# Mamba-2 scan and PReLU block: last six pairs of chunks cut into chunks of 64 tokens, with a pair's outputs, the next pair's gram and its state products in one visit of TensorE

## The chip, the cores and the metric

The kernel runs on one core of one Trainium2 chip. The metric is the device time of one execution in microseconds (us), the median of the runs shown. Before the change three runs took 355.93, 356.24 and 357.10 us, so the median is 356.24 us.

TensorE is the matmul engine (PE in the profile, its weight loads PEld), VectorE is DVE, ScalarE is ACT, GpSimd is POOL, and SyncE (SP) issues most of the DMAs. PSUM is the memory that matmuls write. [...]

## The reference

There are 4 batches, 8 heads, 768 tokens, a head dimension D of 32 and a state dimension N of 16. For each head a decayed linear attention is computed, then all tokens go through a two-layer block with a PReLU:

```python
for c in range(nc):                      # chunks of 32 tokens
    cum = cumsum(log(clip(a)))           # in the chunk
    L = exp(cum_i - cum_j) * (i >= j)
    y_intra = ((C @ B.T) * L) @ x        # the gram C B^T, decayed
    y_inter = (C @ state) * exp(cum)
    state = exp(sum(la)) * state + sum_j(exp(cum_last - cum_j) * B_j x_j)
x = y.transpose(0, 2, 1, 3).reshape(3072, 256)
h = x @ w_in                             # 256 -> 2048
out = (max(h, 0) + alpha * min(h, 0)) @ w_out    # 2048 -> 256
```

The result does not depend on the length of a chunk. A kernel may take 128 or 64 tokens: the work inside a chunk (gram, decay, product with x) grows with its length, and each chunk needs one state at its beginning.

## The kernel before

**Tiling.** The 3072 tokens are 24 chunks of 128 (`Q`), or 12 pairs of chunks (`gp` is 0 to 11, `NP = 12`, three pairs to a batch). Two pairs make a group of 512 tokens (`g` is 0 to 5), the unit of the two-layer block. The scan of a pair has to leave its result, the tile `xT` of its group, before the block begins with that group. The kernel therefore works on group g of the block while it scans the pairs of group g+1 (`nxt = 2g + 2`).

**The block.** From group 1 on, the block uses seven products in place of eight (a Strassen-like scheme with sums of weights and of tokens). `quad(g, z, after, third)` does a quarter of the hidden units, z = 0 to 3. It writes two PSUM tiles, A and Y, from the pool `ps_h`, which has two buffers. A "third" quad also has a tile Z in the pool `ps_s`. The order on each engine is the order of the Python code, since the schedule is manual. A quad runs: A; Y; A again after ScalarE copied A away to `u2` (L1265); VectorE adds `u2` to Y (L1267); A again and Y again; PReLUs on ScalarE (L1224) and VectorE (L1226); four differences on GpSimd (L1288, L1298). Between these stand fifteen places `after(0)` to `after(14)`. There the products of the previous quad with `w_out` (`product`, L1216) and the steps of the scan are put. The tables `with_gram` and `without` (L1502 to 1504) give the places of the products, and `steps` (L1487) those of the scan. At z = 0 from g = 2 on, `combine` joins the products of the group before. Its last two VectorE steps (L1322, L1323) and the two GpSimd steps behind them (L1325, L1326) stand at `after(14)`.

**The scan of a pair.** `pair(gp)` is a generator whose steps are called by `ssm`. In order:

- `added` or `added_halves` multiplies the state input (`bn`, B times its decays, made on GpSimd at L533) with x.
- `states` (L642) carries the state over. GpSimd spreads it over the heads (L645).
- `scan_half` (L561, L567) makes the decays L, by a scan on VectorE of the decay rows that a DMA spread over the partitions (`load_spread`, tile `abc`), with an identity matrix as the other operand. That identity lies in half of a PSUM bank whose other half holds product 5 of the block.
- `spread_c` and `c_decayed` (L679, L682) prepare C. For the later pairs `moved` (L690, L692) also brings C and state to the other 64 partitions.
- `products_bc` (L722) makes the gram on TensorE, into two tiles of `ps_s` and two of `ps_h`. VectorE multiplies it with the decays (L753).
- The outputs are matmuls of C with the state (L779) and of x with the decayed gram (L787), and ScalarE copies them to `xT` (L815).

The last six pairs (`gp >= HALF`, which is 6) already work with the array cut into tiles of 64 rows: tokens 0 to 63 and 64 to 127 of a chunk are two "halves" j. The upper half of the gram has 128 columns, the lower half only 64, so a head takes `SQ` = 192 columns.

**Two visits.** TensorE turns to each of these pairs twice. The gram stands at `after(13)` of an even quad (z = 0 or 2). The outputs stand at `after(5)` of the odd quad that follows, between the products of `u2`'s A and the next use of A, and the state products of the next pair come right behind them.

**Buffers.** `ps_s` and `ps_h` have two banks each, `ps_q` four. `lda` (the tiles `abc`) and `ldx` (x, B, C) have three buffers, `work` two, `czp` one.

Of the kernel before, what the change touches and what calls it, by code (L numbers as in the profile page):

```python
# [22 lines left out]
def kernel(  # L23
# [55 lines left out]
    SQ = Q + HQ  # L79
# [69 lines left out]
    def load_spread(gp, b, c):  # L149

        for w, t in enumerate(loads["p", gp][1] if gp >= HALF else ()):
            rows = scratch["z", b // 2].rearrange("(b h c) t -> b c h t", b=2, h=H)
            for k in range(2):
                nc.sync.dma_start(
                    out=t[HQ * k : HQ * (k + 1), : 4 * SQ].rearrange("p (h t) -> p h t", h=4),
                    in_=rows[b % 2, c + k, 4 * w : 4 * w + 4].unsqueeze(0)
                    .to_broadcast([HQ, 4, SQ]))
# [12 lines left out]
    def load_pair(gp, decays=True, parted=False):  # L170
# [47 lines left out]
        for k in range(2 if gp >= NB else 0):  # L218
            abc.append(lda.tile([P, H * Q], F32, name="abc"))
# [201 lines left out]
    def halve_identity():  # L421

        for s in range(2):
            nc.scalar.copy(
                out=ident_p[0][HQ:].rearrange("p (a s t) -> p s a t", a=2, s=2)[:, s],
                in_=ident[HQ:, HQ * (1 - s) : HQ * (2 - s)].unsqueeze(1).to_broadcast([HQ, 2, HQ]))
# [22 lines left out]
    def rows_clamp(i):  # L449
        rows = loads.pop(("r", i))  # L450
        d0 = prep.tile([RW, SQ], F32, name="r0")
# [5 lines left out]
        if i:  # L457
            nc.vector.tensor_scalar(out=d0[:, Q + 1 :], in0=rows[:, HQ + 1 :], scalar1=1e-6,
                                    scalar2=1.0, op0=ALU.max, op1=ALU.min)
        held[i] = d0  # L460

    def rows_scan(i):

        d0 = held[i]
        nc.vector.memset(d0[:, Q : Q + 1], 0.0)
        pr = prep.tile([RW, Q], F32, name="pr")
        nc.vector.tensor_tensor_scan(out=pr[:, ::-1], data0=d0[:, 1 : Q + 1][:, ::-1],
                                     data1=ends[:RW, ::-1], initial=0.0,
                                     op0=ALU.mult, op1=ALU.add)
        return pr  # L470

    def rows_out(i):


        if i == 0:
# [3 lines left out]
        d0 = held.pop(i)[:, :SQ]  # L479
        rpf = prep.tile([RW, Q], F32, name="rpf")  # L480
        nc.vector.tensor_tensor_scan(out=rpf, data0=d0[:, :Q], data1=zeros[:RW], initial=1.0,
                                     op0=ALU.mult, op1=ALU.add)
        nc.vector.memset(d0[:, :1], 0.0)
# [68 lines left out]
    halved = []  # L552

    def scan_half(dec, abc, k, w):
        dv = dec.rearrange("p k h t -> p k (h t)")
        if ident_p and halved:
            dv = dec.rearrange("p k h t -> p (k h t)")
            for i in range(2):
                s = (2 * w + i) * SQ
                o = (4 * k + 2 * w + i) * SQ  # L560
                nc.vector.tensor_tensor_scan(out=dv[:, o : o + SQ], data0=abc[k][:, s : s + SQ],  # L561
                                             data1=ident_p[0][:, :SQ], initial=0.0,
                                             op0=ALU.mult, op1=ALU.add)
            return
# [6 lines left out]
    def turn_bc(gp):  # L571
# [7 lines left out]
        scan_half(decs[gp], loads["p", gp][1], 0, 0)  # L579

    def pair(gp):
# [5 lines left out]
        half = gp >= HALF  # L587
        dec = decs.pop(gp) if gp in decs else work.tile([P, 2, H, Q], F32, name="dec")
        by_head = dec.rearrange("p k h t -> p (k h t)")[:, : H * SQ].rearrange(
            "p (h t) -> p h t", h=H)  # L590
# [15 lines left out]

        shifted = one.tile([P, 2, P], F32, name="shifted") if half else None

        def added_halves(banks):


            dps = [t[:, : 4 * D].rearrange("p (k m) -> p k m", k=2) for t in banks]
            for j in range(2):
                for r in range(4):
                    rs, hs = slice(32 * r, 32 * r + 32), slice(2 * r * D, 2 * (r + 1) * D)
                    for k in range(nk):
                        ks = slice(HQ * k, HQ * (k + 1))
                        nc.tensor.matmul(dps[k][rs, k], bn[ks, j, rs], xt[ks, j, hs],
                                         start=False, stop=j == 1,
                                         tile_position=(HQ * k, 32 * r),  # L620
                                         skip_group_check=True)
            return dps
# [30 lines left out]
        if fine:  # L653
            bn = bns.pop(gp) if gp in bns else pair_loads(gp)
            if half:
                dps = added_halves(beside.pop(gp))
            else:
                dps = added(beside.pop(gp) if gp in beside else ss_tile()[:, : 2 * Q])
# [26 lines left out]
        def moved():  # L685


            for k in range(2):
                to, frm = (slice(HQ * v, HQ * (v + 1)) for v in (k, 1 - k))
                nc.scalar.copy(out=shifted[to, 0], in_=cd[frm, k])  # L690
                if st[k] is not None:
                    nc.gpsimd.tensor_copy(out=shifted[to, 1], in_=st[k][frm])  # L692

# [4 lines left out]
        if fine:  # L698
            for k in range(2):
                for w in range(2):  # L700
# [5 lines left out]
                    if k == 1 and w == 1:  # L706
                        spread_c()
                        c_decayed()
                        if half:
                            moved()  # L710
# [11 lines left out]
        def products_bc():  # L722
            small = 2 if fine else 3
            gram = {r: ss_tile() if r < small else spare() for r in range(4)}
            for j in range(2 if half else 0):
                for r in range(4):
                    rs = slice(32 * r, 32 * r + 32)
                    for k in range(2):
                        o = gram[r][HQ * k : HQ * (k + 1), : 2 * SQ].rearrange(
                            "p (h t) -> p h t", h=2)  # L730
# [849 lines left out]
```

## Time and profile before

| | |
|---|---|
| median of the three runs | 356.24 us |
| the profiled execution | 357.65 us |
| its span, first to last instruction | 355.9 us |
| TensorE matmuls busy | 349.3 us (98%) |
| VectorE busy | 235.8 us (66%) |
| GpSimd busy | 204.4 us (57%) |
| ScalarE busy | 171.8 us (48%) |
| TensorE's share of the chain that ended last | 89% |
| granted TensorE clock | 1.00 |

The profile comes from one execution. A float32 matmul of the program shows as two records, each with its own weight load. A group line reads "line, engine, operation, output<-inputs, shape, xcount | busy us, mean ns". The chain of waits is followed back from the last instruction. In order of time it shows, for each stretch, which instruction was the one that everything later hung on. A busy TensorE is not necessarily an efficient one, so the timeline of the single records is read as well.

### The profile page before, as it was taken

What the parts mean: (1) busy time and instruction counts of PE and PEld (TensorE: products, weight loads), DVE (VectorE), ACT (ScalarE), POOL (GpSimd) and SP (SyncE); (2) the same over time, 40 slices, a digit from 0 to 9 for tenths busy, and PEclk for the clock granted to TensorE, in tenths of its full rate; (3) what the DMA queues carried; (4) which work ended last, traced back from release to release, by engine and by line L of the source; (5) the groups of instructions that cost most, each with busy time, mean ns of one, the idle gap of its engine ahead of it and who ended that gap; (6) DMA issues with size and microseconds to landing.
All of it is one profiled execution on the core that took longest, in us unless ns stands there. A gap on an engine that the chain in (4) does not pass through costs nothing.

```text
span 355.9 us, 7778 instructions
## 1 busy us (share of the span) xinstructions
PE 349.3 (98%) x2985; PEld 284.4 (80%) x2985; DVE 235.8 (66%) x482; ACT 171.8 (48%) x391; POOL 204.4 (57%) x228
## 2 busy tenths in 40 slices
PE   8899999999999999999999999999999999999996
PEld 4576665578788888888888888888888888888885
DVE  6876986998748756847747856757856633643363
ACT  3477576535355346345345445345445344443431
POOL 6776568589939855725646626637526535434520
PEclk9999999999999999999999999999999999999999
DMA  7899989607345403503423423422001001001102
GB/s 138 182 202 270 329 174 279 148 17 159 106 83 128 102 3 75 104 2 77 78 57 74 86 51 71 85 55 65 11 2 31 0 2 29 2 1 31 31 0 59
DMA packets 105581, 30.24 MB, mean 85 GB/s; under 512 B 79896, under 2 KB 101448, under 8 KB 105544
## 3 DMA queue, kind: packets, MB, share of 16 engines
q1 hardware_dynamic: 103048, 29.43, 36.3%
q10 hardware_dynamic: 2496, 0.32, 0.6%
q8 instruction: 23, 0.38, 0.5%
q14 instruction: 14, 0.11, 0.1%
HBM read 26.32 MB, written 3.42 MB: 84 GB/s over the span
## 4 chain that ended last, share of the span: by engine, by line
PE 89%; SPq 4%; DMA 3%; DVE 2%; ACT 1%; POOL 1%; issue 0%; DVEq 0%; ACTq 0%
PE bank L1216 33%; PE hp L1241 29%; PE bank L1142 6%; PE ss L1241 6%; PE hp L1095 3%; DMA raw<-in_moe_w_in_dram 2%; SPq L192 2%; PE ss L787 1%; PE ss L731 1%; PE hp L1110 1%; PE bank L1209 1%; PE ss L805 1%; PE ss L779 1%; DMA xt<-in_x_dram 1%; SPq L197 1%; PE ss L742 1%
## 5 line engine op out<-in xcount | busy, mean ns | idle before, releaser
L1298 POOL TENSOR_TENSOR gt<-gt 128x512 f32<-128x512 f32 x58 | 74.2, 1279 | 21.1 <-DVE gt L1226 16.3
L1216 PE MATMUL bank<-gt,w_out 128*128 128x256 f32 x320 | 83.5, 381 | 0.0
L1216 PEld LDWEIGHTS bank<-gt,w_out 128*128 128x128 f32 x320 | 60.1, 190 | 9.2 <-issue 1.0
L1288 POOL TENSOR_TENSOR gt<-gt 128x512 f32<-128x512 f32 x20 | 25.4, 1269 | 62.5 <-DVE gt L1226 49.7
L1226 DVE SCALAR_TENSOR_TENSOR gt<-hp,s_mul,gt 128x256 f32<-128x256 f32 x96 | 42.0, 479 | 29.1 <-ACT gt L1224 26.8
L1224 ACT ACTIVATE gt<-hp,s_alpha 128x256 f32<-128x256 f32 x96 | 40.3, 471 | 34.5 <-PE hp L1241 31.4
L1216 PE MATMUL bank<-gt,ws 128*128 128x256 f32 x224 | 55.9, 379 | 0.0
L1216 PEld LDWEIGHTS bank<-gt,ws 128*128 128x128 f32 x224 | 42.3, 190 | 5.6
L1241 PE MATMUL hp<-xs,w_in 128*128 128x256 f32 x160 | 41.9, 384 | 0.0
L1241 PE MATMUL hp<-xs,ws 128*128 128x256 f32 x160 | 41.1, 380 | 0.0
L1267 DVE TENSOR_TENSOR hp<-hp,u 128x512 f32<-128x512 f32 x20 | 14.0, 700 | 35.2 <-ACT u L1265 35.2
L1241 PEld LDWEIGHTS hp<-xs,ws 128*128 128x128 f32 x160 | 30.3, 190 | 4.3 <-POOL xs L1183 0.2
L1241 PEld LDWEIGHTS hp<-xs,w_in 128*128 128x128 f32 x160 | 29.7, 190 | 4.5
L1142 PE MATMUL bank<-w_out,gt 128*128 128x256 f32 x128 | 31.1, 385 | 0.4 <-POOL w_out L330 0.4
L1142 PEld LDWEIGHTS bank<-w_out,gt 128*128 128x128 f32 x128 | 23.6, 190 | 7.2 <-issue 2.9
L1241 PE MATMUL ss<-xT,w_in 128*128 128x256 f32 x96 | 24.6, 379 | 0.0
L645 POOL TENSOR_TENSOR sm<-state,bmask 128x256 f32<-128x256 f32 (+1 forms) x10 | 6.2, 620 | 29.0 <-DVE state L642 29.0
L1095 PE MATMUL hp<-xT,w_in 128*128 128x512 f32 x48 | 22.8, 596 | 0.0
L561 DVE TENSOR_TENSOR_SCAN dec<-abc,bank 128x192 f32<-128x192 f32 x48 | 22.7, 522 | 0.0
L1256 ACT COPY m<-hp 128x512 f32<-128x512 f32 x8 | 4.7, 586 | 35.7 <-PE hp L1241 35.7
L1265 ACT COPY u<-hp 128x512 f32<-128x512 f32 x20 | 11.7, 585 | 19.4 <-PE hp L1241 19.4
L1226 DVE SCALAR_TENSOR_TENSOR gt<-c,s_mul,gt 128x256 f32<-128x256 f32 x40 | 20.6, 555 | 0.0
(232 smaller groups left out, 608.2 us busy)
## 6 DMA issues: line engine op xcount, KB each, us to landing
abc<-z SPq DMA_DIRECT2D x24, 192.0 KB
raw<-in_moe_w_in_dram SPq DMA_DIRECT2D x8, 512.0 KB
raw<-in_moe_w_out_dram SPq DMA_DIRECT2D x8, 512.0 KB
abc<-z SPq DMA_DIRECT2D x8, 512.0 KB
out_dram<-o_sb SPq DMA_DIRECT2D x32, 64.0 KB
nat<-in_B_dram SPq DMA_DIRECT2D x26, 64.0 KB
xt<-in_x_dram SPq DMA_DIRECT2D x12, 128.0 KB
xt<-in_x_dram SPq DMA_DIRECT2D x24, 64.0 KB
```

The source lines that it names most:

```text
L192: eng.dma_start(out=nat[:, i, k].rearrange("p (h n) -> p h n", h=H), in_=src[b, :, ts, :].rearrange("h p n -> p h n"))
L561: nc.vector.tensor_tensor_scan(out=dv[:, o : o + SQ], data0=abc[k][:, s : s + SQ], data1=ident_p[0][:, :SQ], initial=0.0, op0=ALU.mult, op ...
L1095: nc.tensor.matmul(hp, w_in[:, k, f * P : (f + 1) * P], xts[g][:, k], start=(k == 0), stop=(k == KC - 1))
L1142: nc.tensor.matmul(pos[0][t // 2][:, t % 2], gt[:, t * Q : (t + 1) * Q], w_out[:, f], start=(f == 0 and t % 2 == 0), stop=(f == NF - 1), s ...
L1216: nc.tensor.matmul(ms[g][i][:, h], w, blocks[g, z][n][:, p], start=(q == 0 and h == 0), stop=(q == NQ - 1), skip_group_check=True)
L1224: nc.scalar.mul(o[:, p], h[:, p], s_alpha[:, fs[p]])
L1226: nc.vector.scalar_tensor_tensor(out=o[:, p], in0=h[:, p], scalar=s_mul[:, fs[p]], in1=o[:, p], op0=ALU.mult, op1=ALU.max)
L1241: nc.tensor.matmul(to[:, p], w(2 * z + p), b, start=start and p == 0, stop=True, skip_group_check=True)
L1265: nc.scalar.copy(out=u2, in_=A)
L1267: nc.vector.tensor_tensor(out=Y, in0=Y, in1=u2, op=ALU.add)
L1288: nc.gpsimd.tensor_tensor(out=tc_, in0=g22, in1=g12, op=ALU.subtract)
L1298: eng.tensor_tensor(out=o, in0=x0, in1=x1, op=ALU.subtract)
```

## The change

Pairs 6 to 11 go from halves of a 128-token chunk to true chunks of 64 tokens.

1. **Shape.** The decay rows restart every 64 tokens (`rows_scan`, `rows_out`). A head has 128 columns per pair instead of 192 per chunk half. A pair needs one tile `abc` and four scans of 128x256 on VectorE instead of two tiles and eight scans of 128x192. The gram of each half has 128 columns, and the four multiplications are 128x256 instead of 128x384.
2. **States.** There are four states per pair. `state_products` has the same sixteen matmuls, with the sums of the two halves no longer added up. `states_four` has up to four VectorE steps. `carried_four` has eight GpSimd operations on 64 partitions each and two ScalarE copies.
3. **One visit.** `visit(gp)` at `after(13)` of an even quad issues the gram of pair gp+1, two of its four multiplications on VectorE, the outputs of pair gp, the copies to `xT`, and the state products of pair gp+1. The outputs are written to the second half of the two `ps_h` banks whose first half holds gram, the state products to the second half of the two `ps_s` banks. `behind(gp)` at `after(1)` of the odd quad issues the other two multiplications and the states; `carried_four` follows at `after(2)`.
4. **Way in.** Quad (1, 3) becomes a third quad. Pair 5 puts its outputs at `after(6)` there, and its `xT` copies come before the state products of pair 6. `carried_four(6)` follows at `after(11)`, and at `after(13)` a visit with the gram of pair 6 alone and two extra matmuls of ones.
5. **Loads.** From pair 7 on, a pair is loaded one pair earlier than before.

The core of the diff, with the parts of the old path that go left out:

```diff
@@ rows_scan / rows_out
+        n = HQ if i else Q
+        for o in range(0, Q, n):
+            nc.vector.tensor_tensor_scan(out=pr[:, o : o + n][:, ::-1],
+                                         data0=d0[:, o + 1 : o + n + 1][:, ::-1],
...
@@ new functions
+    def scan_four(gp, n):
+        cs = slice(2 * Q * n, 2 * Q * (n + 1))
+        nc.vector.tensor_tensor_scan(out=decays_of(gp)[:, cs], data0=loads["p", gp][1][0][:, cs],
+                                     data1=ident_p[0], initial=0.0, op0=ALU.mult, op1=ALU.add)
+    def c_by_head(gp):
+        czs[gp] = czp.tile([P, 2, 2, Q], F32, name="cz")
+        for i in range(2):
+            nc.scalar.mul(czs[gp][:, i].rearrange("p k t -> p (k t)"),
+                          bcs[gp][:, 2:].rearrange("p k t -> p (k t)"), par[:, i : i + 1])
+    def gram_four(gp, banks, begun=()):
+        cz = czs.pop(gp)
+        for j in range(2):
+            js = slice(HQ * j, HQ * (j + 1))
+            for r in range(4):
...
+                for k in range(2):
+                    o = banks[r][HQ * k : HQ * (k + 1), : 2 * Q].rearrange("p (h t) -> p h t", h=2)
+                    nc.tensor.matmul(o[:, :, js], bcs[gp][rs, k, js], cz[rs, :, k, js],
...
+    def decayed(gp, banks, r):
+        o = decays_of(gp)[:, 2 * Q * r : 2 * Q * (r + 1)]
+        nc.vector.tensor_tensor(out=o, in0=banks[r][:, : 2 * Q], in1=o, op=ALU.mult)
+    def states_four(gp, dps):
...
+            nc.vector.scalar_tensor_tensor(out=to, in0=entering[gp][:, s], scalar=ap[:, e : e + 1],
+                                           in1=new, op0=ALU.mult, op1=ALU.add)
+    def carried_four(gp):
...
+        for k in range(2):
+            to, frm = (slice(HQ * v, HQ * (v + 1)) for v in (k, 1 - k))
+            nc.gpsimd.tensor_tensor(out=cs[to, 0], in0=ct[to, k], in1=ap[to, k], op=ALU.mult)
+            nc.gpsimd.tensor_tensor(out=cd[frm], in0=ct[frm, k], in1=ap[frm, k], op=ALU.mult)
+            nc.scalar.copy(out=cs[to, 1], in_=cd[frm])
...
+            for i, rows in enumerate((to, frm)):
+                nc.gpsimd.tensor_tensor(
+                    out=ss[to, i, js].rearrange("p j (g m) -> p j g m", g=2),
+                    in0=ent[rows, 2 * k + js.start : 2 * k + 2].unsqueeze(2)
...
+    def outputs_four(gp, y, fresh):
+        for i in range(2):
+            for j in range(2):
...
+                            nc.tensor.matmul(y[k][qs, k ^ i, js], ss[ks, i, j, qs], cs[ks, i, js],
...
+        for w in range(2):
+            for j in range(2):
...
+                        nc.tensor.matmul(y[k][qs, w, HQ * j : HQ * (j + 1)],
+                                         xt[ks, j, h * D : (h + 1) * D],
+                                         decays_of(gp)[ks, o : o + HQ], start=False, stop=True,
...
+    def visit(gp):
+        nxt = gp + 1
+        banks = {0: ss_tile(), 1: spare(), 2: ss_tile(), 3: spare()}
+        if nxt < NP:
+            begun = (1, 3) if gp < HALF else ()
+            for r in begun:
...
+            gram_four(nxt, banks, begun)
+            for r in (1, 3):
+                decayed(nxt, banks, r)
+        if gp >= HALF:
+            y = [banks[r][:, 2 * Q :].rearrange("p (k t) -> p k t", k=2) for r in (1, 3)]
+            outputs_four(gp, y, nxt >= NP)
...
+            for k in range(2):
+                nc.scalar.copy(out=xts[g][:, :, (q + k) * Q : (q + k + 1) * Q], in_=y[k])
+            if nxt < NP:
+                beside[nxt] = [banks[r][:, 2 * Q :] for r in (0, 2)]
+                state_products(nxt, beside[nxt])
+        visits[gp] = banks
+    def behind(gp):
+        nxt, banks = gp + 1, visits.pop(gp)
+        if nxt < NP:
+            for r in (0, 2):
+                decayed(nxt, banks, r)
+            if gp >= HALF:
+                states_four(nxt, beside.pop(nxt))
@@ order of the steps
+    def thirds(g, z):
+        return 2 * g + 2 >= NP or z % 2 == 0 or (g, z) == (1, 3)
+    def sixth(z, j):
...
+        if (z, j) == (3, 6):
+            state_products(n, beside[n])
+            states_four(n, beside.pop(n))
+        if (z, j) == (3, 11):
+            carried_four(n)
+        if (z, j) == (3, 13):
+            visit(n - 1)
+        if (z, j) == (3, 14):
+            behind(n - 1)
+            turn_bc(n + 1)
+    def fours(gp, odd, j):
...
+        if not odd and j == 13:
+            visit(gp)
+        if odd and j == 1:
+            behind(gp)
+        if odd and j == 2 and gp + 1 < NP:
+            carried_four(gp + 1)
+        if odd and gp + 2 < NP:
+            if j == 5:
+                turn_bc(gp + 2)
+                scan_four(gp + 2, 0)
+            if j in (12, 14):
+                scan_four(gp + 2, 1 if j == 12 else 2)
...
+            late = 6 if (g, z) == (1, 3) else 5
...
+            if z % 2 and j == late and gp < HALF:
+                for p in (0, 1, 0, 1):
+                    ssm(gp + p)
+            if gp == HALF - 1:
+                sixth(z, j)
+            if HALF <= gp < NP:
+                fours(gp, z % 2, j)
+            if z % 2 and j == 9 and gp + (2 if gp < HALF - 1 else 3) < NP:
+                load_pair(gp + (2 if gp < HALF - 1 else 3))
...
-        quad(g, z, after, nxt >= NP or z % 2 == 0)
+        quad(g, z, after, thirds(g, z))
```

## The prediction

> **What bounds the kernel now.** The page comes first: TensorE is busy for 98% of the span, and the chain of waits gives it 89%. The second answer read is the list of TensorE's waits. It names six, 3.1 us together, and all six belong to lines of the start, before group 1. So from group 1 on, where the change lies, TensorE never idles. What is added to its queue, or keeps it waiting, lengthens the kernel; what other engines gain does not count.
>
> ```profile
> PE 349.3 (98%) x2985; PEld 284.4 (80%) x2985; DVE 235.8 (66%) x482; ACT 171.8 (48%) x391; POOL 204.4 (57%) x228
> PE 89%; SPq 4%; DMA 3%; DVE 2%; ACT 1%; POOL 1%; issue 0%; DVEq 0%; ACTq 0%
> ```
>
> Third, the chain in order of time around pair 6 (start, length, what). Four records of a full stream last 0.86 us, 0.216 each.
>
> ```profile
> 144.89 1.29 PE bank L1216 x6
> 146.18 0.38 PE ss L731 x4
> ...
> 147.02 1.06 PE bank L1216 x4
> ...
> 151.53 0.86 PE bank L1216 x4
> 152.40 0.24 PE ss L779 x4
> ...
> 154.13 1.92 PE hp L1241 x8
> ```
>
> The gram takes 146.18 to 147.02, and the first four full records after it 1.06 in place of 0.86: 1.04 us. The outputs with the state products take 152.40 to 154.13, plus 1.92 less 1.73: 1.92 us. Read alike, all six grams cost 1.03 and the outputs of pairs 6 to 11 cost 1.93, 1.86, 1.95, 1.93, 1.86, 1.61 (the last has no state products). Together 6.2 + 11.1 = 17.3 us.
>
> Fourth, the timeline around the gram of pair 7, and around the u copy of the quad behind pair 6's gram.
>
> ```profile
> 173.25 0.45 PE L731 MATMUL ss<-cz,bc 32*64 32x256 f32 x4
> 173.73 0.29 PE L731 MATMUL ss<-cz,bc 32*64 32x128 f32 x4
> 173.84 0.29 PE L731 MATMUL ss<-cz,bc 32*64 32x128 f32 x4
> 173.87 0.29 PE L731 MATMUL hp<-cz,bc 32*64 32x128 f32 x4
> 174.23 1.02 DVE L753 TENSOR_TENSOR dec<-hp,dec 128x384 f32<-128x384 f32 x2 [2.15 <-PE hp L731]
> ```
>
> ```profile
> 148.12 0.42 DVE L1322 TENSOR_TENSOR c<-u,bank 128x256 f32<-128x256 f32 x1
> 148.46 0.42 DVE L1323 TENSOR_TENSOR c<-bank,u 128x256 f32<-128x256 f32 x1
> 151.57 0.58 ACT L1265 COPY u<-hp 128x512 f32<-128x512 f32 x1 [1.14 <-PE hp L1241]
> ```
>
> To be seen: eight array tiles work at once, and a round of 128 columns takes 0.11 us (173.73 to 173.84). VectorE starts 0.07 us after the gram's modelled end. A 128x256 operation on PSUM takes 0.42, the next starts 0.34 after it. The u copy waits for TensorE alone.
>
> [...] weight loads stop for 0.33 us before each visit, of which I count 0.31 as lost. [...] of the last outputs' 1.61 us, 0.31 is the drain and 0.43 the four 128-column rounds of L779; 0.87 is left for the eight rounds of L787, half with 128 columns and half with 64, which is 0.109 each. [...]
>
> **The change part by part.**
>
> *The visit's wait.* The outputs go to the second half of the two banks whose first half holds gram, so as built their first matmul waits for both `decayed(1)` and `decayed(3)`. Queued behind it: the whole of TensorE. From the visit's start: 0.31 drain; the gram's four rounds start at 0, 0.16, 0.27 and 0.38 (the first pair spaced 0.05 wider than its columns, as in L731), plus 0.05 within a round and 0.27 to the end, near 0.69 (bank 1's part 0.66); VectorE starts at 0.74; two multiplications, 0.34 + 0.42, end at 1.49; TensorE follows 0.05 later (VectorE's L887 to TensorE's L929 took that). Resumption at 0.31 + 1.49 + 0.05 = 1.85 us, where the gram's columns alone would end at 0.31 + 0.43. After `combine` (pairs 6, 8, 10) VectorE is at L1319 and L1320 until 147.10, 1.29 after the visit's start, so both multiplications are 0.24 later: 2.09.
>
> *The visit's columns.* State: 32 matmuls of 64 columns (before, 16 of 128); x: 32 of 64 (before, 16 of 128 and 16 of 64); each is 8 rounds counting both passes. At 0.109 a round that is 0.87 + 0.87. State products and way out as before: 1.95 - 1.61 = 0.34. A merged visit costs 1.85 + 2.08 = 3.93, after `combine` 4.17. The bound from below is 0.054 a round, the columns alone, as if rounds were proportional: 0.87 less. I take 0.109, because L787 measures it.
>
> *Sum of visits.* 3 x 4.17 + 2 x 3.93 = 20.4. The last visit has no gram: 0.31 + 0.87 + 0.87 = 2.05. The visit with pair 6's gram alone: 0.31 + 0.43 + 0.43 for the matmuls of ones + 0.13 = 1.30. Together 23.7 against 17.3: **+6.4** (bound below +1.2).
>
> *Pair 5.* Its state products for pair 6 now stand behind the two `xT` copies, in the same bank. Matmul end and handover about 0.3, two copies 0.27 + 0.38, less the drain that is there anyway: **+0.9** (0.5 to 1.1).
>
> *The copies of `carried_four` on ScalarE.* They stand ahead of the u copy (L1265's work), and the next use of A on TensorE waits for that. They wait for GpSimd. Quads behind visits 6, 8 and 10: `combine`'s L1322 needs product 4, which now comes after the whole visit. From the visit's end: product 4 done 1.24; L1322, L1323 end 2.04; GpSimd's L1325, L1326 (0.73 each) end 3.54; then two products 64x128, two 64x256, two 64x128 before the second copy can start. The trace shows no GpSimd product on 64 partitions. I take the time of 128 partitions with the same row length (L645: 0.45 and 0.73), with starts 0.41 and 0.70 apart: 6.58. Copies end 6.95, u copy 7.50. TensorE, through five pieces of 0.86 and product 2, wants A at 5.18: **2.4 us** of idling, 1.8 for pair 9, whose first two spreads are 64x128. Before, this quad had the outputs (1.9 us) in this place. Sum **+6.6**. The bound below is half the GpSimd times: 2.4. Quads behind visits 7, 9, 11 have no `combine`: second copy by 3.95, u copy wanted at 4.73, so no hold; but the u copy ends at 5.32 against 5.18: +0.1 each, **+0.3** (0 to 0.6).
>
> *`carried_four(6)`.* Its copies stand ahead of the next quad's copy from Z to A. GpSimd's last difference (L1298) ends 4.2 after a gram visit's start (150.03 against 145.81), 3.65 without the `bn` step there; six products (four of 64x128) bring the second copy to 6.5, the copy to A to 7.1. TensorE wants A at 1.30 + 3.5 pieces = 4.3: **+2.8** (bound below 1.6).
>
> *At nothing.* Four scans in place of eight, 128x256 in place of 128x384, and fewer DMA bytes all lie on engines and queues with idle time; if that cover went they would be gains of VectorE, not of TensorE. SyncE's loads move a pair earlier, and the buffers they need are freed by the visit before. The third quad (1, 3) has the same matmuls. C's spread on ScalarE delays an even quad's u copy to 4.32, wanted by 4.75.
>
> **Sum:** 6.4 + 0.9 + 6.6 + 0.3 + 2.8 = +17.0 us. The profiled execution took 357.65 (span 355.9), so 374.7 (span 372.9); that execution is 1.4 above the median of 356.24, which gives **373.2 us**.
>
> **Rivals.**
>
> *Short matmuls are cheap.* Rounds of 64 columns at 0.054: 5.2 us less, 368.0. For it: some state products (L618) are that close. Against it: L787. If GpSimd's narrow operations are half as well: 1.2 + 0.5 + 2.4 + 1.6 = +5.7, 362.
>
> *ScalarE's copies hold nothing.* If the GpSimd work before the second copy is short enough, only the visits remain: 373.2 - 6.6 - 2.8 = 363.8. Against it: that would take the six products from 3.0 to some 0.6 us.
>
> *Not slower: TensorE's own work decides.* If VectorE's multiplications were in time, a visit would save one drain, a way out and columns: at 0.054 a round 0.31 + 0.43 + 0.86 + 0.34 = 1.95 against 2.96, so about 5 us in five visits, 351. It decides where the wait inside the visit is shorter than the 1.0 us saved and nothing holds ScalarE. The two multiplications with their handovers alone are 1.1.
>
> **Chances.** The likeliest case 0.60; between it and 364 (one of the first two rivals, or half of each) 0.28; both, 360 to 364, 0.06; the last rival 0.04; no change 0.02. A measurement of this kernel tells about 0.3% from no change (1.1 us): slower 0.94, same 0.02, faster 0.04. The range reaches from 361.5, where all lower bounds meet, to 376.5, with rounds of 64 columns 0.03 dearer than 0.109.
>
> **What would show it.** Right: TensorE waits for VectorE's multiplications in five visits, some 1.1 us each; 16 rounds near 0.11 between resumption and state products; TensorE waits for ScalarE's u copy in three quads, near 2.4 us, and once for the copy to A; ScalarE's copies behind GpSimd. Wrong: no such wait in the list, or the outputs of a visit under 1.5 us. It would fail most if narrow GpSimd products were quick.

## The result, and the profile after

The changed kernel takes **389.76 us** (median of 4 runs, 388.39 to 390.28); the kernel before took 356.31 us beside it. The ratio is **1.093**, 95% interval 1.0896 to 1.0963. The direction was forecast, the size was not: 373.2 us, at most 376.5. The profiled execution took 389.65 us with a span of 387.9, so 32.0 us of span have to be found.

The page of the changed kernel: engines, TensorE's granted clock in 40 slices, instruction queue 8, taken for TensorE's (25 packets for its 3197 records and 3197 weight loads), and the chain.

```profile
PE 357.9 (92%) x3197; PEld 288.6 (74%) x3197; DVE 227.6 (59%) x471; ACT 171.3 (44%) x389; POOL 219.9 (57%) x254
PEclk9999999999998998999999998999998999999999
q8 instruction: 25, 0.41, 0.4%
PE 78%; DVE 7%; POOL 6%; issue 3%; DMA 2%; ACT 2%; SPq 1%; POOLq 0%; DVEq 0%
```

TensorE's share fell from 98% to 92%, and on the chain from 89% to 78%. Its busy time grew by 8.6 us all the same, although the waits are not in it: the row of the clock shows where, in four slices with an 8. The list of TensorE's waits, its seven largest lines from group 1 on (behind the arrow the releaser, which is what ended the wait; then us in total, times, longest; `issue` means that the profile shows no releaser):

```profile
PE hp L1317 <- ACT u L1341: 7.1, 3, 2.6
PE hp L676 <- DVE dec L604: 3.8, 5, 1.1
PE bank L1292 <- DVE dec L581: 3.4, 1, 3.4
PE bank L1292 <- issue: 3.1, 2, 1.7
PE hp L1317 <- ACT hp L1328: 2.1, 1, 2.1
PE ss L876 <- DVE gt L1302: 1.2, 1, 1.2
PE ss L1317 <- DVE dec L855: 1.0, 1, 1.0
```

Three of these seven were forecast: the u copy (L1341), the gram's multiplications (`decayed`, L604) and the copy from Z to A (L1328). The other four were not.

Each full 128x128 matmul of the quads has its counterpart in the other trace. Its start after the change less its start before is a delay, and the delay grows in steps. The ledger of the span, each step's growth, and what the forecast had for it:

| where | measured, us | forecast, us |
|---|---|---|
| before 80 us, outside the change | 0.3 | 0 |
| product 5 waits for pair 6's scan | 3.5 | 0 |
| four stretches at half clock | 6.9 | 0 |
| pair 5's part of quad (1, 3) | 3.9 | 0.9 |
| copy from Z to A behind `carried_four(6)` | 2.4 | 2.8 |
| u copy, three quads after `combine` | 7.9 | 6.6 |
| u copy, the other three | 0.3 | 0.3 |
| visits: drain, columns, wait for VectorE | 3.3 | 6.4 |
| visits: pauses without a releaser | 3.3 | 0 |
| sum | 31.8 (of 32.0) | 17.0 |

**The hold on ScalarE**, as forecast: the chain of waits in order of time after the visit of pair 6.

```profile
166.69 0.73 POOL c L1401
167.43 0.69 POOL c L1402
168.11 0.42 POOL cd L650
...
168.60 0.45 POOL other L651
...
169.13 0.72 POOL sm L656
...
169.90 0.72 POOL sm L656
...
170.68 0.45 POOL cd L650
...
171.19 0.46 POOL other L651
...
171.68 0.30 ACT cd L652
...
172.00 0.59 ACT u L1341
```

GpSimd works through `combine`'s two sums and then six products of 64 partitions, 0.45 and 0.72 us each, as the forecast had taken them from 128 partitions (0.45 and 0.73). Only then can ScalarE make the second copy (L652), and the u copy behind it, which waits for nothing else. TensorE starts again at 172.63.

**The scan in the way.** The timeline around 116 us of the changed kernel:

```profile
115.46 0.59 PE L1292 MATMUL bank<-gt,ws 128*128 128x256 f32 x2
115.51 0.38 ACT L421 COPY bank<-ident_q 128x256 f32<-128x256 f32 x1
115.70 2.07 DVE L1302 SCALAR_TENSOR_TENSOR gt<-c,s_mul,gt 128x256 f32<-128x256 f32 x2
117.70 1.09 DVE L561 STREAM_TRANSPOSE bc<-nat 128x512 f32<-128x512 f32 x1
118.64 0.62 DVE L581 TENSOR_TENSOR_SCAN dec<-abc,bank 128x256 f32<-128x256 f32 x1
119.41 1.63 PE L1292 MATMUL bank<-gt,ws 128*128 128x256 f32 x4 [3.36 <-DVE dec L581]
```

`scan_four` reads the identity from the half of the PSUM bank (a tile of 128x512 float32) beside the half that product 5 fills. At `after(8)` it stands ahead of product 5 (`after(9)`), behind a `prelu` and a transposition on VectorE, and TensorE waits for it all, 3.36 us. The four records of product 5 then take 1.63 us in place of 1.03: the granted clock is 0.50 from 119.8 us on.

**The pause without a releaser.** Visit 7 is `visit(7)`, with the outputs of pair 7; the others are numbered alike. The timeline of TensorE at its end:

```profile
193.04 1.11 PE L676 MATMUL hp<-cd,sm 64*32 64x64 f32 x60 [0.52 <-DVE dec L604]
...
194.01 0.82 PE L686 MATMUL hp<-dec,xt 64*32 64x64 f32 x61
194.63 0.47 PE L617 MATMUL ss<-xt,bn 64*32 64x64 f32 x24
196.84 1.13 PE L1292 MATMUL bank<-gt,w_out 128*128 128x256 f32 x4 [1.74 <-issue]
```

No engine is waited for. In the stretch from 194.2 to 195.4 us the view of the DMA shows one packet of queue 8 and nothing else:

```profile
DMA packets 1, 0.02 MB, mean 14 GB/s; under 512 B 0, under 2 KB 0, under 8 KB 0
q8 instruction: 1, 0.02, 5.2%
```

The packet, taken to bring instructions to TensorE since the queue has one to some 256 of TensorE's records and weight loads, is recorded from 194.30 to 195.30. TensorE goes on 1.5 us after that. What happens in between, the trace does not show.

### The profile page after: what moved, and what is told of

Its sections match the earlier page's. It is cut to its first block, busy times and chain, and to the rows that moved or that the text cites. A ratio compares the mean times of both kernels' runs of the same rounds, so it can differ in the third digit from the quotient of the medians.

```text
span 387.9 us, 8209 instructions
## 1 busy us (share of the span) xinstructions
PE 357.9 (92%) x3197; PEld 288.6 (74%) x3197; DVE 227.6 (59%) x471; ACT 171.3 (44%) x389; POOL 219.9 (57%) x254
## 4 chain that ended last, share of the span: by engine, by line
PE 78%; DVE 7%; POOL 6%; issue 3%; DMA 2%; ACT 2%; SPq 1%; POOLq 0%; DVEq 0%
PE bank L1292 28%; PE hp L1317 23%; PE bank L1218 6%; PE ss L1317 5%; PE hp L1171 4%; PE hp L1186 1%; PE hp L676 1%; DMA nat<-in_B_dram 1%; POOL sm L656 1%; DVE gt L1302 1%; PE hp L686 1%; DMA nat<-in_C_dram 1%; POOL gt L1374 1%; POOL other L651 1%; PE bank L1285 1%
## 5 line engine op out<-in xcount | busy, mean ns | idle before, releaser
L1292 PE MATMUL bank<-gt,w_out 128*128 128x256 f32 x320 | 85.2, 386 | 3.1 <-issue 3.1
L1292 PEld LDWEIGHTS bank<-gt,w_out 128*128 128x128 f32 x320 | 60.9, 193 | 12.6 <-issue 4.1
L1292 PE MATMUL bank<-gt,ws 128*128 128x256 f32 x224 | 57.3, 384 | 3.4 <-DVE dec L581 3.4
L1292 PEld LDWEIGHTS bank<-gt,ws 128*128 128x128 f32 x224 | 43.2, 194 | 9.8 <-POOL gt L1364 3.7
L1317 PE MATMUL hp<-xs,w_in 128*128 128x256 f32 x160 | 43.2, 394 | 7.1 <-ACT u L1341 7.1
L1317 PE MATMUL hp<-xs,ws 128*128 128x256 f32 x160 | 41.9, 385 | 2.8 <-ACT hp L1328 2.1
L1317 PEld LDWEIGHTS hp<-xs,w_in 128*128 128x128 f32 x160 | 30.4, 194 | 13.1 <-ACT u L1341 9.0
L1317 PEld LDWEIGHTS hp<-xs,ws 128*128 128x128 f32 x160 | 30.5, 192 | 7.6 <-POOL sm L656 2.5
L1317 PE MATMUL ss<-xT,w_in 128*128 128x256 f32 x104 | 27.7, 390 | 1.3 <-DVE dec L855 1.0
L1317 PEld LDWEIGHTS ss<-xT,w_in 128*128 128x128 f32 x104 | 20.1, 196 | 4.8 <-issue 2.0
L1351 DVE TENSOR_TENSOR c<-hp,m 128x512 f32<-128x512 f32 x20 | 13.7, 686 | 15.9 <-PE hp L1317 15.9
L1317 PE MATMUL hp<-xT,ws 128*128 128x256 f32 x80 | 22.4, 406 | 0.0
L554 DVE TENSOR_TENSOR_SCAN dec<-abc,bank 128x256 f32<-128x256 f32 x32 | 19.3, 664 | 0.0
L1328 ACT COPY hp<-ss 128x512 f32<-128x512 f32 x13 | 7.4, 570 | 26.0 <-PE ss L1317 26.0
```

The source lines that it names most:

```text
L554: nc.vector.tensor_tensor_scan(out=dv[:, k, hs], data0=abc[k][:, hs], data1=ident_p[0], initial=0.0, op0=ALU.mult, op1=ALU.add)
L1292: nc.tensor.matmul(ms[g][i][:, h], w, blocks[g, z][n][:, p], start=(q == 0 and h == 0), stop=(q == NQ - 1), skip_group_check=True)
L1317: nc.tensor.matmul(to[:, p], w(2 * z + p), b, start=start and p == 0, stop=True, skip_group_check=True)
L1328: nc.scalar.copy(out=A, in_=Z)
L1351: nc.vector.tensor_tensor(out=c22, in0=A, in1=m5, op=ALU.add)
```

## The experiments

Theory after the result: the holds on ScalarE and the wait for VectorE are as forecast, and four things were left out, namely a scan ahead of product 5, half clock after pauses, pair 5's part in its new form of quad, and TensorE running out of instructions in dense visits. The chief rival: these are the same lateness of VectorE and GpSimd seen in several places, and removing one only shows the next. No kernel below leaves out any part of the computation. All times are medians, and ratios are to the kernel before the change. That kernel, run beside each batch (e1 to e4; c1 to p1; g1 to g3), had medians of 356.36, 357.19 and 356.45 us, so a difference between batches is good to about 1 us.

**e1_scan: the scan behind product 5.**

```diff
-        if (z, j) in ((2, 8), (2, 11), (3, 2), (3, 3)):
-            scan_four(n, {(2, 8): 0, (2, 11): 1, (3, 2): 2, (3, 3): 3}[z, j])
+        if (z, j) in ((2, 10), (2, 12), (3, 2), (3, 3)):
+            scan_four(n, {(2, 10): 0, (2, 12): 1, (3, 2): 2, (3, 3): 3}[z, j])
```

> Only the first two scans of pair 6 are moved, from after(8) and after(11) to after(10) and after(12) of quad 2 of group 1, behind product 5. Theory: in the changed kernel TensorE's product 5 waits 3.4 us at 116 us because the scan reads the identity from the other half of the PSUM bank that product 5 fills, and the pause then costs one 3.4 us stretch at half clock (1.7 us). Both go: 389.8 - 3.5 - 1.7 = 384.6 us, and the list of TensorE's waits has no scan (line of scan_four) any more. Rival: VectorE, or the load of pair 6, is late anyway, and the next user of VectorE's work (pair 5's gram) waits in its place: 388 us or more.

Measured: 384.23 us, ratio 1.0795 (1.0741 to 1.085). TensorE's timeline, at the same place:

```profile
114.92 1.68 PE L1292 MATMUL bank<-gt,ws 128*128 128x256 f32 x6
116.43 0.25 PE L503 MATMUL ss<-ident,pr 96*128 96x96 f32 x1
```

Product 5's records now follow without a gap and at full clock. From there on the kernel is some 5 us earlier than the changed one (0.5 are lost again at pair 5's gram). The medians differ by 5.5, and the theory holds: only the place of the scans was changed.

**e2_direct: no ScalarE copy in `carried_four`.**

```diff
-        cd = one.tile([P, Q], F32, name="other")
...
-            nc.gpsimd.tensor_tensor(out=cd[frm], in0=ct[frm, k], in1=ap[frm, k], op=ALU.mult)
-            nc.scalar.copy(out=cs[to, 1], in_=cd[frm])
+            nc.gpsimd.tensor_tensor(out=cs[to, 1], in0=ct[frm, k], in1=ap[frm, k], op=ALU.mult)
```

> carried_four's second product is written by GpSimd straight to the other 64 partitions, so the ScalarE copy behind it is gone; the rest is the changed kernel. Theory: that copy, standing ahead of the u copy and of the copy from Z to A, makes TensorE wait 8.1 us (three quads) and 2.4 us (one quad), and three of these four pauses bring a stretch at half clock, 1.7 us each. All go: 389.8 - 8.1 - 2.4 - 5.1 = 374.2 us. Rival: GpSimd itself or VectorE behind the visit is what is late, and the copies only stand in the record: 385 us or more, with the same quads waiting for another instruction.

Measured: 377.13 us, ratio 1.0569 (1.0533 to 1.0606). From group 1 on no wait for ScalarE is left among TensorE's waits; the first three lines are

```profile
PE hp L674 <- DVE dec L604: 3.8, 5, 1.1
PE bank L1290 <- issue: 3.7, 2, 2.0
PE bank L1290 <- DVE dec L581: 3.4, 1, 3.4
```

GpSimd's product takes as long as before (0.45 us), so the rival is out: it was the order on ScalarE. The gain is 12.6 in place of 15.6 us. In the profiled execution 0.9 us are lost before 80 us, where nothing was changed, and one stretch at half clock (1.7 us) is new, behind the pause for instructions at 190 us, which grew to 2.0.

**e3_third: quad (1, 3) in its old form.**

```diff
-        return 2 * g + 2 >= NP or z % 2 == 0 or (g, z) == (1, 3)
+        return 2 * g + 2 >= NP or z % 2 == 0
```

> Quad 3 of group 1 keeps the form it had in the kernel before (Z in the hp bank, not in an ss bank); the rest is the changed kernel. Theory: this form is what makes pair 5's part of the quad wait (1.05 us for the gram's multiplications, 1.23 us for the bank of pair 5's outputs): 389.8 - 2.3 = 387.5 us, both waits gone from the list. Rival: the waits come from pair 5's place among VectorE's work and stay, 389 to 390 us; or the visit with pair 6's gram finds the hp banks taken and waits in their place, over 390 us.

Measured: 387.94 us, ratio 1.0865 (1.0823 to 1.0907). The waits of L876 and of L1317 for L855 are gone, as the theory has it, but two lines show that part of the rival is true as well:

```profile
PE hp L1317 <- ACT hp L1328: 3.0, 1, 3.0
PE hp L704 <- DVE gt L1302: 0.4, 1, 0.4
```

The visit with pair 6's gram waits 0.4 for a bank, and the copy from Z to A is waited for 0.9 longer: TensorE is earlier, GpSimd is not. The time, 1.8 below the changed kernel, whose own four runs lie 1.9 apart, does not decide between them. The run c2_four tests it without ScalarE's copies.

**e4_first: outputs ahead of the gram in the visit.**

```diff
-                                             start=fresh and i == j == 0, stop=False,
+                                             start=fresh and i == 0 and j == (k == 0 and of_four(gp)[0]), stop=False,
...
-            gram_four(nxt, banks, begun)
-            for r in (1, 3):
-                decayed(nxt, banks, r)
         if gp >= HALF:
             y = [banks[r][:, 2 * Q :].rearrange("p (k t) -> p k t", k=2) for r in (1, 3)]
-            outputs_four(gp, y, nxt >= NP)
+            outputs_four(gp, y, True)
+        if nxt < NP:
+            gram_four(nxt, banks, (1, 3))
+            for r in (1, 3):
+                decayed(nxt, banks, r)
+        if gp >= HALF:
```

> In the visits of pairs 6 to 10 the outputs are issued ahead of the next pair's gram and start their banks themselves, so nothing in the visit waits for VectorE. Theory: a visit then has its columns only, 0.3 + 0.65 + 0.67 + 0.43 + 0.33 + 0.1 = 2.5 us in place of 3.5, so five visits give 5 us: 384.8 us, and the waits of the state matmuls for the multiplications (3.8 us in the list) are gone. Rival: a denser visit runs out of fetched instructions (two visits of the changed kernel show 1.4 and 1.7 us without any releaser while a packet of the instruction queue arrives), so pauses without releaser grow and take back 2 to 5 us: 387 to 390 us.

Measured: 385.77 us, ratio 1.0815 (1.0765 to 1.0866). The five waits for `decayed` are gone and the undisturbed visits take 2.5 us (3.4 to 3.7 in the changed kernel). The gain of 4.0 us is between the two expectations, and so is the trace:

```profile
PE hp L1319 <- ACT u L1343: 7.7, 4, 2.6
PE bank L1294 <- issue: 2.9, 2, 1.8
PE hp L598 <- issue: 0.8, 1, 0.8
```

A pause without a releaser appears in a third visit (8), and the wait for the u copy takes back a little. So the wait inside a visit was real and worth about 1 us, but a third visit now pauses.

**c1_three: e1, e2 and e4 together.** The edits are those shown.

> Three of the edits together: pair 6's scans behind product 5, GpSimd's product written straight to the other partitions, outputs ahead of the gram in the visits of pairs 6 to 10. Theory: the three holds are separate, so their gains add: scan and its half clock 5.2, the holds on ScalarE with theirs 15.5, five visits from 3.5 to 2.5 us 5.2, less 1.2 for longer pauses without releaser: 389.8 - 24.7 = 365.1 us, up to 367 if a pause without releaser brings a stretch at half clock. Rival: the waits overlap or the next one is close behind (the visits' gain went into the u copies' waits when done alone), so that no more than e2's time less 5 is reached: 372 us or more.

Measured: 366.11 us, ratio 1.0258 (1.0223 to 1.0294). The gains add: 23.7 of the 24.7 us, where the three runs alone gained 5.5, 12.6 and 4.0. No stretch at half clock is left within the span. Of TensorE's waits from group 1 on:

```profile
PE bank L1292 <- issue: 3.1, 2, 1.7
PE ss L876 <- DVE gt L1302: 1.2, 1, 1.2
PE ss L1317 <- DVE dec L855: 0.9, 1, 0.9
...
PE hp L598 <- issue: 0.8, 1, 0.8
...
PE ss L617 <- issue: 0.3, 1, 0.3
```

The last of these stands before pair 6's state products, behind the copies, and belongs to no visit. The pauses in visits are 1.7, 1.4 and 0.8: 3.9 us.

**c2_four: and quad (1, 3) in its old form.**

> The three edits of the run beside it, and quad 3 of group 1 in its old form. Theory: pair 5's two waits (1.05 and 1.23 us) go without ScalarE's copies to give the gain back: 2.3 us below the run beside it, near 363 us. Rival: as when done alone, the wait for pair 6's banks takes the place of most of it: less than 1 us below.

Measured: 364.24 us, ratio 1.0204 (1.0169 to 1.024): 1.9 below the run beside it. In the profiled executions 1.5 us are won up to the visit with pair 6's gram, and 0.7 later by shorter pauses for instructions, which the edit does not explain. With ScalarE's copies gone the quad's form is thus worth about 1.5 of its two waits' 2.3 us. The visit with the gram of pair 6 becomes 1.1 us longer (2.35 against 1.25), with 0.4 of waiting, so part of the rival is true.

**f1_shift: more instructions ahead of visit 6.** In the visit with pair 6's gram, on top of the three edits (TensorE has 3293 records in place of 3197, and as many weight loads):

```diff
+            for r, k in [(r, k) for r in (0, 2) for k in range(2)] * (12 if begun else 0):
+                rs = slice(32 * r, 32 * r + 32)
+                nc.tensor.matmul(banks[r][HQ * k : HQ * (k + 1), 2 * Q : 2 * Q + HQ],
+                                 warm[rs].to_broadcast([32, HQ]), warm[rs].to_broadcast([32, HQ]),
+                                 start=True, stop=True, tile_position=(32 * r, HQ * k),
+                                 skip_group_check=True)
```

> The three edits, and 48 matmuls of ones (64 columns on 32 rows, into an unused half bank) in the visit with pair 6's gram alone; their result is not used. They are 192 more instructions for TensorE, so every later visit begins at another place in the packets of 256 instructions that TensorE's instructions arrive in. Theory (fetch): visits 7 and 10, which began 77 to 79 instructions past a multiple of 256 and ran dry in each kernel so far, now begin at 13 to 15 and don't pause; visit 8, now at 101, pauses some 1.3 to 1.9 us. Pauses without releaser: from three (4.4 us) to one, for 1 to 2 us of added matmuls: 1 to 2 us below the run without them. Rival: the pauses belong to what visits 7 and 10 do, and stay where they were: 1 to 2 us above it.

Measured: 365.3 us, ratio 1.0253 (1.0202 to 1.0305). Where each visit begins, counted in records of TensorE and its weight loads and taken modulo 256, and behind the colon how long it takes in us:

```
visit        6          7          8          9          10
three edits  13: 2.51   79: 4.38   165: 3.81  7: 2.51    77: 4.24
shifted     206: 2.51   16: 2.61   102: 4.20  200: 2.51  14: 2.61
```

Visits 7 and 10 lost their pauses without any change in what they do, and visit 8 has its pause at another instruction, the state products. TensorE's timeline, visit 8 of the shifted kernel:

```profile
209.59 0.33 PE L617 MATMUL ss<-xt,bn 64*32 64x64 f32 x12
211.21 0.41 PE L617 MATMUL ss<-xt,bn 64*32 64x64 f32 x20 [1.29 <-issue]
```

That is the fetch theory's forecast to the visit, and the rival is out. The time alone would not show it: by the trace the pauses shrink by 2.9 us and the added matmuls cost 1.6, and the 0.8 between the medians lie within the scatter of the four runs (364.68 to 367.32).

The records say it more sharply. In the twelve profiled executions from the changed kernel to g3_both the visits have 25 pauses of this kind with over 0.5 us between two starts. In each of them TensorE stops with 3521, 4033, 4289 or 5313 records started, always 193 past a multiple of 256, whatever instruction comes next. It goes on 1.2 to 1.6 us after a packet of queue 8 has landed.

**p1_early: pair 6's state products ahead of the `xT` copies.**

```diff
         if (z, j) == (3, 6):
-            state_products(n, beside[n])
             states_four(n, beside.pop(n))
...
-                for p in (0, 1, 0, 1):
+                for n, p in enumerate((0, 1, 0, 1)):
                     ssm(gp + p)
+                    if n == 0 and gp == HALF - 1:
+                        state_products(HALF, beside[HALF])
```

> The three edits, and pair 6's state products are told off ahead of the two copies of pair 5's outputs, so they no longer wait for ScalarE; TensorE's order is the same. Theory: the 0.3 us pause ahead of them and the second change of mode go, 1.09 us become 0.35: 0.7 us below the run with the three edits. Rival: the copies of pair 5's outputs then wait for these products and the quads that need pair 5 wait in turn: no gain.

Measured: 365.18 us, ratio 1.0231 (1.0193 to 1.027): 0.9 below the run with the three edits. In the trace the products cost 0.47 in place of 1.09, so the edit is worth 0.6 there. The pauses for instructions in visits 7 and 10 are 1.1 us shorter in this execution, though each visit begins at the same record as before: their length varies from execution to execution.

**g1_pad, g2_split, g3_both: the best that these edits give.** g1_pad has all the edits above. g2_split has them without the added matmuls and with each visit in two, the outputs at `after(13)`, the gram and the state products at `after(14)`. g3_both has the added matmuls, and visit 8 alone in two:

```diff
         if not odd and j == 13:
-            visit(gp)
+            visit(gp, not (gp == 8))
+        if not odd and j == 14 and gp + 1 < NP and (gp == 8):
+            grams(gp)
```

(`grams`, not shown, is the gram, its two multiplications and the state products of `visit`; in g2_split the condition on `gp` is always true.)

> All the edits so far together: the three, quad 3 of group 1 in its old form, pair 6's state products ahead of the copies, and the 48 added matmuls (their result is not used). Theory: the gains add. From 366.1 us: 1.9 for the quad's form, 0.9 for the state products, 0.8 for the shift: 362.5 us, one pause without releaser left (in visit 8). Rival: the gains of pair 5's part are the same microseconds twice: 364 us.

> Without the added matmuls, and each visit of pairs 6 to 10 in two again: the outputs at after(13), the next pair's gram and state products at after(14), product 4 between them. Theory: a visit more costs the second drain and way out, about 0.45 us, 2.2 us for five; the dense part is 256 instructions at most, then 0.9 us of product 4, so the three pauses for instructions (4.7 us with the three edits) shrink to 1 us or less: 363.3 - 3.7 + 2.2 = 361.8 us. Rival: the pauses stay, as the instructions are as many: 365 us.

> As the first of these three runs, with the 48 added matmuls, and only visit 8 in two. Theory: visit 8's pause (1.6 us) goes for 0.45 us: no pause without releaser is left from pair 6 on: 362.5 - 1.2 = 361.3 us. It remains above the kernel before, since what was won in the visits, some 2.3 us, is less than pair 6's gram alone (1.4), the added matmuls (1.5) and what pair 5's part of group 1 has lost. Rival: the pause only moves to the gram behind product 4: 362.5 us.

Measured: 361.93 us (ratio 1.0154, 1.0112 to 1.0196), 362.79 us (1.0173, 1.0138 to 1.0207), **360.68 us** (1.0105, 1.0068 to 1.0142). The gains add again: g1_pad is 0.6 below its forecast. g2_split is 1.0 above its own. There the pauses for instructions shrink to

```profile
PE ss L617 <- issue: 0.9, 2, 0.5
```

at the price of a second way in and out in each visit, expected at 0.45 us. In g3_both visit 8 keeps 0.5 us of pause, so the rival of the last expectation is partly true. The best of them is faster than the changed kernel by 29.1 us and still about 1% slower than the kernel before.

## Why the prediction was wrong, step by step

**What held.** TensorE is the bound, and its pauses lengthen the kernel (31.8 of 32.0 us in the ledger). The hold on ScalarE: 6.6 forecast, 7.9 measured (2.8, 2.3 and 2.8), and e2_direct shows the mechanism. The copy to A: 2.8 against 2.4. Pair 6's state products behind the copies: 0.9 forecast, 0.7 in the breakdown below, 0.6 won back in the trace of p1_early. GpSimd on 64 partitions took 0.45 and 0.72 us, on 128 partitions 0.45 and 0.73: the bound from above was the right one. The terms that the forecast had come to 14.6 us measured (3.3, 0.7, 7.9, 0.3 and 2.4) against 17.0. So the direction was no luck. That the two sums lie close is partly luck, since the visits were costed 3.1 too high and the u copy 1.3 too low.

**The visit's wait** is there in five visits. It is smaller than forecast, since VectorE starts 0.83 us after the visit's start (1.00 after `combine`) and not at 1.05 and 1.29: the gram's first record follows the full stream after 0.09, where the forecast put the whole 0.31 that it counts for the stop of the weight loads (0.33 at each of the visits 6 to 11 here). TensorE has passed its wait for both multiplications 1.6 to 1.9 us after the visit's start, not at 1.85 and 2.09. In visits 7, 8 and 10 the first state matmul waits for the first multiplication alone, and only the next ones for the second.

**The visit's columns: a term mis-sized.** A round of eight 64-column matmuls was taken at 0.109. But this is the mean of L787's mixed rounds, half of them with 128 columns, so it cannot show that short ones cost as much: that was the author's estimate. The last visit of the changed kernel measures it alone:

```profile
314.58 0.80 PE L676 MATMUL hp<-cd,sm 64*32 64x64 f32 x60
```

The 64 records of the state matmuls (60 in this line) start within 0.64 us, eight to a round: 0.08. The same for x: 0.085. The truth lay between the two bounds, 0.054 and 0.109. The last visit costs 1.61, not 2.05. Two ends of the forecast's range are also a little off: its lower bounds add up to 5.7, which is 361.9 and not 361.5, and 0.03 more on 16 rounds in six visits is 2.9, which is 376.1 and not 376.5.

**The step that failed: "At nothing", and pauses priced at their length alone.** Two sentences of "At nothing" were wrong.
- Fewer scans were costed at nothing, as VectorE has idle time. But a scan also reads a PSUM bank, and TensorE waited 3.36 us for one in the other half of the bank it fills: what counts is where the scan stands against TensorE's use of the bank. The scan's new place was never checked against product 5. The forecast did let work in one half of a bank wait for work in the other, but only in the banks of the visit and of pair 5's products. Price: 3.5 us, and 1.7 more that the ledger counts with the clock (e1_scan).
- "The third quad (1, 3) has the same matmuls." It has, but its Z lies in an `ss` bank, and pair 5's gram and outputs want these banks in the same quad. Of the 3.9 us of pair 5's part, 1.2 are the first of Z's matmuls waiting for the gram's multiplications, 1.6 the outputs waiting for Z to be read, 0.4 Z of the next quad waiting for pair 6's gram, 0.7 the state products. Of the first three, c2_four wins back 1.5.

**Left out: the clock.** Pauses of TensorE were priced at their length. The kernel before could not show another price: after 100 us no two of TensorE's starts there lie more than 0.32 us apart, and the granted clock is 1.00 over the whole span. The forecast itself counted pauses of 2.4, 1.8, 2.4 and 2.8 us. The changed kernel has five intervals of 2.1 to 3.7 us between two starts after 100 us (3.74, 2.53, 2.94, 2.39 and 2.93), and all but the third are followed by a stretch at half clock. Its busy times and granted clock (third to last column) in four stretches, of which the third is the one without:

```profile
119.90:123.20 3.30, 3.30 (x10) 2.57 (x10) 0.82 (x2) 0.68 (x4) 1.03 (x2) 0.50 0.95 98
150.60:153.90 3.30, 3.30 (x9) 2.66 (x8) 1.09 (x2) 0.81 (x3) 0.34 (x1) 0.50 0.51 78
172.60:176.00 3.40, 3.37 (x16) 2.98 (x17) 3.23 (x6) 1.33 (x4) 0.62 (x1) 1.00 0.00 0
232.50:235.90 3.40, 3.40 (x9) 2.66 (x8) 2.43 (x4) 0.14 (x1) 0.28 (x1) 0.50 0.00 0
```

At half clock TensorE starts 9 or 10 records in such a stretch, at full clock 16. A stretch lasts 3.41 us, so it costs 1.7; in the ledger four cost 6.9. In c1_three, where no two starts after 100 us lie more than 1.92 apart, no stretch is left. The pause ahead of 172.6 was 2.6 us long and has no such stretch behind it, that of 2.0 ahead of 232.5 has one.

**Left out: instructions.** The forecast did not ask how TensorE's instructions arrive. In the changed kernel TensorE and its weight loads have 6394 records, and queue 8 brings 25 packets, 0.41 MB: 16.4 KB and 256 records a packet. In f1_shift it is 26 packets for 6586 records (253 each), in the kernel before 23 for 5970 (260). In visit 7, 3009 records have started when the packet before begins and 3521 when TensorE stops, which is 512 more. In that visit the 256 records ahead of the stop start within 1.4 us. The next packet lands only 1.8 us after the first of them, and the instructions behind it start at 3.3 us. There TensorE started a packet's worth of records faster than the next packet came. Price: 3.3 us, and 3.9 where nothing else slows the visit (c1_three).

So of the 14.8 us by which the ledger exceeds the forecast, 10.2 belong to two prices that the forecast left out (6.9 clock, 3.3 instructions), 6.5 to "At nothing" (3.5 and 3.0 of pair 5's part), 1.3 to the u copy, less 3.1 of visits and 0.4 of the copy to A that were costed too high. The remaining 0.3 lie before the change.

**The last rival** ("TensorE's own work decides", about 5 us faster) fails on more than its waits. Without the wait a visit costs 2.5 us against 2.96 for the two of before, so five give 2.3 us, not 5; pair 6's gram needs a visit of its own (1.45 us), the pauses for instructions take more than the rest. What stays open: some 0.5 us around pair 5's gram in the kernels with the scan moved, which no run takes apart.

## What to carry to other kernels

When a full engine is made to wait, price the pause and what follows it: here a pause of 2.1 to 3.7 us between two starts was mostly (16 of 23) followed by 3.4 us at half clock. An instruction that costs its own engine nothing must be followed to every bank and queue it stands in, and against the engine that is full (one scan held TensorE for 3.36 us). Packing many small instructions into one visit saves entries (at each of them the weight loads stopped for 0.33 us), but in these traces TensorE's instructions came at about 256 to a packet, and visits of 367 and 383 records within some 2.3 us could run dry here.

## What the runs showed of the hardware that was not expected

- **Half clock after pauses.** In the eleven profiled executions of the changed kernel and the experiments up to g2_split, TensorE has 23 intervals of 2.1 to 3.7 us between two starts after 100 us, and 16 of them are followed by a half-clock stretch (granted clock 0.50 for 3.41 us, once 6.83). None of the 40 from 1.0 to 2.04 is. Whether a pause is followed by one changes from run to run: the four runs of e1_scan lie between 381.28 us at a mean granted clock of 0.991 and 386.92 us at 0.981.
- **Running dry.** A dense visit of some 370 records paused when it began 76 to 102 records past a multiple of 256 (1.0 to 2.1 us), and one of 384 also at 165; it did not at 6 to 16 or at 197 to 206, apart from two visits with some 0.3 us. In the changed kernel, whose visits wait in the middle, the one at 165 does not pause; there the packet landed (220.77) before the visit began (221.29), and why it came earlier is not shown. All 25 pauses in visits stand 193 records past a multiple of 256, and the record behind each starts 2.4 to 4.0 us after the one 256 records before it.
- **GpSimd across partitions.** A product of 64x128 written to other partitions than its inputs lie on takes as long (0.45 us, e2_direct) as one that stays (0.45 us, L650 and L651 of the changed kernel).
